# Whole-row loads of w_in, the first xT copies on GpSimd's queue, y copied by ScalarE alone, and another order of the first turn

## The chip, the cores and the metric

The kernel runs on one core of one Trainium2 chip. The metric is the device time of one execution in microseconds (us). Of the kernel before there are three timed executions, 340.52, 340.43 and 339.38 us, with a median of 340.43 us, and a fourth, profiled execution, from which every line of the profile comes.

## The reference, cut to what matters

A gated linear recurrence over 4 batches, 8 heads, 768 steps and 48 columns per head feeds a gated state-space block:

```python
for t in range(S):                                     # attention, per batch and head
    state = alpha[:, :, t, :, None] * state + k_t (outer) v_t
    y[:, :, t] = q_t @ state
x = y.transpose(0, 2, 1, 3).reshape(B, S, H * D)        # 4 x 768 x 384
proj = x @ w_in                                         # 384 x 1024
val, gate = proj[..., :512], proj[..., 512:]
h = exp(A_log) * h + val                                # running over the steps
out = (silu(gate) * hs) @ w_out                         # 512 x 384
```

`w_in` and `w_out` arrive as 64-bit floats (3.15 MB and 1.57 MB) and are turned into 32-bit ones on the chip.

## The kernel before, in words

The work is cut into N = 12 groups of 256 steps (three for each batch), each of two chunks of 128 steps. The function `fast` writes the order of every engine's instructions by hand; no scheduler moves them. An engine executes its own list strictly in order and waits, at each instruction, for what that one needs.

**The groups.** For a group m, q, k, v and alpha are loaded (groups 0 to 2 in "natural" layout by `load_natural`, L417, and turned by TensorE transposes `tn`, L563 and L574; later groups by `load_raw`, L396, and turned on VectorE, L597). VectorE runs two scans over alpha (`prod`, L606, and `inv`, L618) and scales q and k into Z (L580 or L629). TensorE makes the scores (L652) and the transposed keys (`tp`, L642), ScalarE and GpSimd mask them into A (L658 and L659; the other half is VectorE's L660), and TensorE makes y from A and v (L671), the state st (L692) and the part carried over from the chunk before (L682). `join(m)` (L697) copies the two halves of y out of PSUM into xT, one by ScalarE (L701) and one by VectorE (L702), and then moves six strips of 16 partitions within xT by six small DMAs (L705), three for each of the two engines named in its argument.

**The turns.** The loop at L821 runs over the groups' second part. Turn n multiplies xT of group n with w_in in four column blocks (`project(n, cc)`, L720: six matmuls for the values pv, six for the gates pg), runs the recurrence on VectorE (L727), applies Silu on ScalarE (`sg`, L732), multiplies the two on GpSimd (`f`, L733) and multiplies f with w_out (`output`, L741, sixteen matmuls). The last four of these wait for the fourth f. In the same turn the attention of group n+1 (scores to `join(n+1)`) and the scans of group n+2 are threaded between the four projections. Before the loop, group 0 and a part of group 1 are done.

**The weights.** `load_w` (L442) fetches w_in in three units by columns: unit 0 and unit 1 with 128 columns each for the values and the gates, unit 2 with 256 of each, every unit by eight DMAs (four of 48 rows times 3, four of 16 rows times 3), and w_out in two halves by one DMA of 128 partitions each (L456). The split into 48 and 16 rows is there because each head's 48 columns sit on the partitions 0 to 47 and 64 to 111, and what is left on 48 to 63 and 112 to 127. `convert(i)` (L506) makes 32-bit floats of one piece: one ScalarE instruction (`wr`, L518), two on VectorE (L519, L521) and one addition on GpSimd (L523), each over 768 elements a partition; `wr` has one buffer. There are six such pieces, four of w_in, one for each column block, and two of w_out. In turn 0 the six conversions stand at L814, L850, L867, L872, L893 and L895. `check_w` (L525) later reduces each loaded unit to a largest and a smallest value on VectorE, two reductions in each turn from turn 3 on.

**The queues.** SyncE (SP) issues nearly all loads in order. Each DMA's completion uses one of eight semaphores in rotation, shared by SP's and ScalarE's DMAs, and a DMA's issue waits for the one that used its semaphore before. So a load on SP can wait for a small xT copy that ScalarE issues later in the turn. In the profile, SPq and ACTq are SP and ScalarE issuing DMAs. `Lnnn` is a line of the kernel before.

Of the kernel before, what the change touches and what calls it, by code (L numbers as in the profile page):

```python
# [346 lines left out]
def fast(  # L347
# [87 lines left out]
    w_out = const.tile([C, NI, DM], FP32, name="w_out")  # L435

    W_UNITS = [(0, C), (C, C), (2 * C, 2 * C)]
    NW = 5
    wbits = [const.tile([C, NK, 2, w, 2], U32, name=f"wbits{i}") for i, (_, w) in enumerate(W_UNITS)]
    wbits += [const.tile([C, 2, 1, DM, 2], U32, name=f"wbits{i}") for i in range(3, NW)]  # L440

    def load_w(i, *engines):  # L442
        if i < 3:
            col, w = W_UNITS[i]
            src = moe_w_in.bitcast(U32)
            n = 0
            for rows in (((0, D, 0, D), (64, D, 4 * D, D)), ((D, R, 3 * D, R), (64 + D, R, 7 * D, R))):
                for vg in range(2):
                    for row, size, first, step in rows:
                        engines[n % len(engines)].dma_start(  # L450
                            out=wbits[i][ds(row, size), :, vg].rearrange("p kk n two -> p kk (n two)"),
                            in_=src[ds(first, NK * step), ds(2 * (vg * DI + col), 2 * w)]
                            .rearrange("(kk p) n -> p kk n", p=step)[0:size])
                        n += 1
        else:
            engines[0].dma_start(  # L456
                out=wbits[i].rearrange("p cc one n two -> p cc (one n two)"),
                in_=moe_w_out.bitcast(U32)[ds(2 * C * (i - 3), 2 * C)].rearrange("(cc p) n -> p cc n", p=C))
# [47 lines left out]
    def convert(i, part=0):  # L506

        if i < 3:
            bits = wbits[i][:, :, :, ds(part * C, C)]
            w = w_in[:, :, :, ds(W_UNITS[i][0] + part * C, C)]  # L510
        else:
            bits = wbits[i]
            w = w_out[:, ds(2 * (i - 3), 2), None, :]
# [4 lines left out]
        nc.scalar.activation(r, lo, AF.Copy, scale=2.0 ** -29)  # L518
        nc.vector.tensor_scalar(out=t, in0=hi, scalar1=3, scalar2=0x3FFFFFFF,  # L519
                                op0=ALU.logical_shift_left, op1=ALU.bitwise_and)  # L520
        nc.vector.scalar_tensor_tensor(out=t, in0=hi, scalar=0xC0000000, in1=t,  # L521
                                       op0=ALU.bitwise_and, op1=ALU.bitwise_or)
        return lambda: nc.gpsimd.tensor_tensor(out=w.bitcast(I32), in0=w.bitcast(I32), in1=r, op=ALU.add)  # L523

    def check_w(i):  # L525
        hi = wbits[i].rearrange("p a b n two -> p (a b n) two")[:, :, 1].bitcast(FP32)
        nc.vector.tensor_reduce(out=wmax[:, i:i + 1], in_=hi, axis=mybir.AxisListType.X, op=ALU.max,
                                apply_absolute_value=True)
        yield
        nc.vector.tensor_reduce(out=wmin[:, i:i + 1], in_=hi, axis=mybir.AxisListType.X, op=ALU.min,  # L530
                                apply_absolute_value=True)
        yield
# [164 lines left out]
    def join(m, engines):  # L697

        y = ys.pop(m)
        xT = xTs[m] = p2.tile([C, 4, GC], FP32, tag="xT", name="xT")  # L700
        nc.scalar.activation(xT[:, 1::2], y[1], AF.Copy)  # L701
        nc.vector.tensor_copy(out=xT[:, 0::2], in_=y[0])  # L702
        for s in range(2):
            for a in range(NK):
                engines[s].dma_start(out=xT[ds(64 * s + D, R), a], in_=xT[ds(64 * s + R * a, R), 3])  # L705
# [76 lines left out]
    load_w(2, SP)  # L782
    pair("a", 2, SP, SP)
    for i in range(3, NW):
        load_w(i, SP)
    pair("k", 2, SP, SP)
    pair("q", 2, SP, SP)

    warm = ps_mm.tile([C, 4, C], FP32, tag="mm", name="warm")
    for _ in range(5):  # L790
        nc.tensor.matmul(warm, ident, ident[:, None, :].to_broadcast([C, 4, C]), start=True, stop=True)
# [7 lines left out]
    for c in range(G):  # L799
        keys(0, c)  # L800
    for c in range(G):
        masks(0, c)
# [10 lines left out]
    join(0, (ACT, ACT))  # L813
    convert(0)()  # L814
    k_times, q_times = natural_qk(1, "k"), natural_qk(1, "q")
    for _ in steps:
        pass

    checks = itertools.chain.from_iterable(check_w(i) for i in range(NW))
    value = None  # L820
    for n in range(N):  # L821
# [24 lines left out]
        if n == 0:  # L846
            for c in range(G):
                k_times(c)
                q_times(c)
            convert(1)()  # L850
# [20 lines left out]
        if n == 0:  # L871
            convert(2, 1)()  # L872
# [3 lines left out]
        gated(n, 2, *pj)  # L876
        if not nat:
            go(2)
        if att:
# [6 lines left out]
            join(m, (ACT, ACT) if n < 2 else (SP, ACT))  # L886
        pj = project(n, 3)
        gated(n, 3, *pj)
        if nat:
            natural_alpha(n + 2)  # L890
            check_alpha(n + 2)
            go(2)
            convert(3)()  # L893
            go(1)
            convert(4)()  # L895
# [50 lines left out]
```

## Time and profile before

| what | value |
|---|---|
| median of three timed executions | 340.43 us (339.38 to 340.52) |
| profiled execution, its own time | 343.17 us |
| its span, first to last instruction | 341.4 us |
| mean granted TensorE clock | 0.935 of full |
| TensorE (PE) matmul busy | 297.5 us, 87% of the span |
| VectorE (DVE) busy | 232.3 us, 68% |
| GpSimd (POOL) busy | 105.5 us, 31% |
| ScalarE (ACT) busy | 91.7 us, 27% |
| DMA | 39.71 MB in 68269 packets, mean 116 GB/s |

All times in the profile's rows are us from the span's start. In a timeline row stand the start, the duration, the engine, the line, the operation, what it writes and reads with its shape, and how often; the bracket at the end gives how long the engine had been idle before and what ended that. In a row of the windows stand the stretch and its length, then the busy time of PE, PEld (TensorE's weight loads), DVE, ACT and POOL with the number of instructions, then the granted clock, the DMA share and GB/s. The profiled execution lies 2.74 us above the median of the timed ones, and 1.77 us of it lie outside the span.

### The profile page before, as it was taken

What the parts mean: (1) busy time and instruction counts of PE and PEld (TensorE: products, weight loads), DVE (VectorE), ACT (ScalarE), POOL (GpSimd) and SP (SyncE); (2) the same over time, 40 slices, a digit from 0 to 9 for tenths busy, and PEclk for the clock granted to TensorE, in tenths of its full rate; (3) what the DMA queues carried; (4) which work ended last, traced back from release to release, by engine and by line L of the source; (5) the groups of instructions that cost most, each with busy time, mean ns of one, the idle gap of its engine ahead of it and who ended that gap; (6) DMA issues with size and microseconds to landing.
All of it is one profiled execution on the core that took longest, in us unless ns stands there. A gap on an engine that the chain in (4) does not pass through costs nothing.

```text
span 341.4 us, 5950 instructions
## 1 busy us (share of the span) xinstructions
PE 297.5 (87%) x2341; PEld 234.5 (69%) x2341; DVE 232.3 (68%) x256; ACT 91.7 (27%) x188; POOL 105.5 (31%) x97
## 2 busy tenths in 40 slices
PE   3983869249997996899999999999999999999992
PEld 3572658116873883687886887878878788787771
DVE  3855671460896696389799899997998969643110
ACT  4161321311411421131411424214124152121111
POOL 6022272040251340072360611813516027041020
PEclk9997878757998999699999999999999999999997
DMA  9994996641406927980592956908739330100101
GB/s 134 181 170 91 187 265 137 167 69 48 113 0 145 239 55 140 225 141 12 154 205 65 239 76 163 202 15 216 144 99 222 60 94 3 38 22 13 47 4 54
DMA packets 68269, 39.71 MB, mean 116 GB/s; under 512 B 47364, under 2 KB 66952, under 8 KB 68232
## 3 DMA queue, kind: packets, MB, share of 16 engines
q1 hardware_dynamic: 65744, 38.30, 55.7%
q10 hardware_dynamic: 2488, 0.94, 1.3%
q8 instruction: 20, 0.33, 0.5%
q14 instruction: 17, 0.14, 0.1%
HBM read 33.33 MB, written 4.72 MB: 111 GB/s over the span
## 4 chain that ended last, share of the span: by engine, by line
PE 65%; DMA 10%; DVE 9%; SPq 6%; issue 4%; ACTq 2%; POOL 1%; ACT 1%; DVEq 0%; POOLq 0%
PE pv L720 17%; PE o L741 16%; PE pg L720 15%; PE sc L652 5%; DMA wbits<-in_moe_w_in_dram 5%; PE y L671 5%; PE y L682 2%; PE st L692 2%; SPq L420 2%; SPq L450 2%; ACTq L705 2%; PE tp L642 2%; DMA raw_k<-in_k_dram 2%; DVE prod L606 2%; DMA raw_q<-in_q_dram 1%
## 5 line engine op out<-in xcount | busy, mean ns | idle before, releaser
L733 POOL TENSOR_TENSOR f<-sg,hh 128x256 f32<-128x256 f32 x48 | 57.6, 1201 | 174.7 <-ACT sg L732 146.4
L720 PE MATMUL pv<-xT,w_in 128*128 128x256 f32 x288 | 77.7, 409 | 14.4 <-POOL w_in L523 10.1
L741 PE MATMUL o<-w_out,f 128*128 128x384 f32 x192 | 69.5, 516 | 13.9 <-POOL w_out L523 11.5
L720 PEld LDWEIGHTS pv<-xT,w_in 128*128 128x128 f32 x288 | 55.8, 201 | 28.5 <-POOL w_in L523 10.9
L720 PE MATMUL pg<-xT,w_in 128*128 128x256 f32 x288 | 73.3, 392 | 0.0
L741 PEld LDWEIGHTS o<-w_out,f 128*128 128x128 f32 x192 | 38.2, 201 | 40.0 <-POOL w_out L523 12.8
L720 PEld LDWEIGHTS pg<-xT,w_in 128*128 128x128 f32 x288 | 57.2, 199 | 8.6
L732 ACT ACTIVATE sg<-pg 128x256 f32<-128x256 f32 x48 | 18.4, 384 | 134.2 <-PE pg L720 84.2
L727 DVE TENSOR_TENSOR_SCAN hh<-a_dec,hh,pv 128x256 f32<-128x256 f32 x32 | 23.5, 735 | 42.5 <-PE pv L720 40.6
L659 POOL TENSOR_TENSOR A<-A,mask 128x512 f32<-128x512 f32 x24 | 32.0, 1354 | 30.2 <-ACT A L658 30.2
L606 DVE TENSOR_TENSOR_SCAN prod<-aT,first 128x1024 f32<-128x1024 f32 x12 | 32.8, 2734 | 0.1
L618 DVE TENSOR_TENSOR_SCAN inv<-aT,last 128x1025 f32<-128x1025 f32 x12 | 31.0, 2584 | 0.4
L652 PE MATMUL sc<-Z 48*128 48x128 f32 x384 | 25.1, 278 | 0.7 <-DVE Z L580 0.7
L671 PE MATMUL y<-A,v 128*64 128x128 f32 x384 | 23.9, 274 | 1.6 <-POOL A L659 1.6
L652 PEld LDWEIGHTS sc<-Z 48*128 48x128 f32 x384 | 22.7, 188 | 3.6 <-issue 2.2
L745 ACT ACTIVATE o_sb<-o 128x384 f32<-128x384 f32 x24 | 11.8, 491 | 48.6 <-PE o L741 48.6
L727 DVE TENSOR_TENSOR_SCAN hh<-a_dec,pv 128x256 f32<-128x256 f32 x16 | 10.9, 679 | 19.6 <-PE pv L720 19.4
L671 PEld LDWEIGHTS y<-A,v 128*64 128x64 f32 x384 | 20.7, 137 | 2.3 <-POOL A L659 2.1
L660 DVE TENSOR_TENSOR A<-sc,mask 128x512 f32<-128x512 f32 x24 | 16.4, 689 | 6.9 <-PE sc L652 6.6
L597 DVE STREAM_TRANSPOSE aT<-raw_a 128x1024 f32<-128x1024 f32 x9 | 18.3, 2038 | 0.0
L597 DVE STREAM_TRANSPOSE Z<-raw_q 128x1024 f32<-128x1024 f32 x9 | 18.3, 2036 | 0.0
L597 DVE STREAM_TRANSPOSE Z<-raw_k 128x1024 f32<-128x1024 f32 x9 | 18.2, 2018 | 0.0
(82 smaller groups left out, 249.8 us busy)
## 6 DMA issues: line engine op xcount, KB each, us to landing
raw_k<-in_k_dram SPq DMA_DIRECT2D x24, 192.0 KB, 5.0
raw_q<-in_q_dram SPq DMA_DIRECT2D x24, 192.0 KB, 5.2
v<-in_v_dram SPq DMA_DIRECT2D x24, 192.0 KB, 4.4
out_dram<-o_sb SPq DMA_DIRECT2D x24, 192.0 KB, 1.9
raw_a<-in_alpha_dram SPq DMA_DIRECT2D x23, 192.0 KB, 4.0
raw_a<-in_alpha_dram SPq DMA_DIRECT2D x18, 176.0 KB, 4.0
raw_k<-in_k_dram SPq DMA_DIRECT2D x18, 176.0 KB, 5.1
raw_q<-in_q_dram SPq DMA_DIRECT2D x18, 176.0 KB, 4.0
```

What stands on the lines that cost most here:

```text
L597: nc.vector.transpose(out=to.rearrange("p h (c j) -> p h j c", j=NT), in_=raw_bufs[m % NR][name].rearrange("p h (j d) -> p h j d", d=D)[:, ...
L606: nc.vector.tensor_tensor_scan(out=prod, data0=aT[:, 0:4 * GC], data1=first.rearrange("p h n -> p (h n)"), initial=0.0, op0=ALU.mult, op1= ...
L618: nc.vector.tensor_tensor_scan(out=inv[:, ::-1], data0=aT[:, ::-1], data1=last.rearrange("p h n -> p (h n)")[:, 0:4 * GC + 1][:, ::-1], in ...
L652: nc.tensor.matmul(sc[i][:, p, :], Z[rows, p, 1, cols], Z[rows, p, 0, cols], start=True, stop=True)
L659: nc.gpsimd.tensor_mul(A[:, 1], A[:, 1], mb)
L660: nc.vector.tensor_mul(A[:, 0], sc[0], mb)
L671: nc.tensor.matmul(ys[m][i][ds(64 * s, 64), e, ds(c * C, C)], v_sb[:, c, 2 * p + i, :], A[:, i, p, :], start=(c == 0 and e == 0), stop=Fal ...
L720: nc.tensor.matmul(pj, w_in[:, kk, vg, ds(cc * C, C)], xT[:, kk, :], start=(kk == 0), stop=(kk == NK - 1))
L727: nc.vector.tensor_tensor_scan(out=hh, data0=a_dec[:, cc:cc + 1].to_broadcast([C, GC]), data1=pv, initial=prev_h[cc][:, GC - 1:GC] if g el ...
L732: nc.scalar.activation(sg, pg, AF.Silu)
L733: nc.gpsimd.tensor_mul(fs[n][:, cc, :], sg, hh)
L741: nc.tensor.matmul(os[c], fs[n][:, cc, ds(c * C, C)], w_out[:, cc, :], start=(cc == 0), stop=(cc == NI - 1))
```

## The change

Five things are changed, all in `fast`:

- `load_w_in` fetches w_in once, in four DMAs of whole rows (48 or 16 partitions, 3 rows of 8 KB each), where there were 24. They stand where unit 0's eight DMAs stood on SP. w_out follows behind k and q of group 1, v of group 1 behind that, and then a, k and q of group 2.
- `join(0)` and `join(1)` issue their six small DMAs on GpSimd's queue and no longer on ScalarE's; `join(2)` uses SP and ScalarE, as the later groups do in both kernels.
- Both copies of y in `join` are ScalarE's, in every group.
- `convert` works on one column block of w_in or one half of w_out at a time (i = 0 to 5) and `wr` has two buffers. The conversions are put in other places of turn 0: the fourth block behind project(0, 1), both halves of w_out behind project(0, 2), where they had stood behind project(0, 3) and the scans of group 2. The scaling of k and q of group 1 (L580) goes ahead of project(0, 0); it stood behind it. Group 0's masks go ahead of its keys. A second set of five matmuls on a constant (`warm`) is put behind group 0's y.
- `check_w` goes by rows of w_in (three units of 1024 elements a partition) and halves of w_out (two of 768); before, it was units of 768, 768, 1536, 768 and 768.

The diff, cut to its core:

```diff
-    W_UNITS = [(0, C), (C, C), (2 * C, 2 * C)]
...
+    bits_in = const.tile([C, NK, 2 * DI, 2], U32, name="bits_in")
+    bits_out = const.tile([C, NI, DM, 2], U32, name="bits_out")
+    def load_w_in(engine):
+        for row, size, first, step in ((0, D, 0, D), (64, D, 4 * D, D), (D, R, 3 * D, R), (64 + D, R, 7 * D, R)):
+            engine.dma_start(out=bits_in[ds(row, size)].rearrange("p kk n two -> p kk (n two)"),
+                             in_=moe_w_in.bitcast(U32)[ds(first, NK * step)]
+                             .rearrange("(kk p) n -> p kk n", p=step)[0:size])
...
-        r = p1.tile([C, x, y, z], I32, tag="wr", name="wr")
+        r = p2.tile([C, x, y, z], I32, tag="wr", name="wr")
...
         nc.scalar.activation(xT[:, 1::2], y[1], AF.Copy)
-        nc.vector.tensor_copy(out=xT[:, 0::2], in_=y[0])
+        nc.scalar.activation(xT[:, 0::2], y[0], AF.Copy)
...
-    load_w(0, SP)
+    load_w_in(SP)
     pair("k", 1, SP, SP)
     pair("q", 1, SP, SP)
-    load_w(1, SP)
+    for i in range(2):
+        load_w_out(i, SP)
     load_v(1, SP)
...
-    join(0, (ACT, ACT))
+    join(0, (nc.gpsimd, nc.gpsimd))
     convert(0)()
+    warm()
     k_times, q_times = natural_qk(1, "k"), natural_qk(1, "q")
     for _ in steps:
         pass
+    for c in range(G):
+        k_times(c)
+        q_times(c)
...
         if n == 0:
-            convert(2, 1)()
+            convert(3)()
...
         pj = project(n, 2)
         gated(n, 2, *pj)
+        if n == 0:
+            convert(4)()
+            convert(5)()
...
-            join(m, (ACT, ACT) if n < 2 else (SP, ACT))
+            join(m, (nc.gpsimd, nc.gpsimd) if n == 0 else (SP, ACT))
...
-            convert(3)()
-            go(1)
-            convert(4)()
```

SP's loads behind v of group 0, before (`wbits_88` to `wbits_90` are the three units of w_in, `wbits_91` and `wbits_92` the halves of w_out; `raw_k_83`, `raw_q_82` and `v_85` belong to group 1, `raw_a_78` here to group 2):

```order
L429 DMA v_84<-in_v_dram 128x8x48 x2
L450 DMA wbits_88<-in_moe_w_in_dram 48x3x256 x4
L450 DMA wbits_88<-in_moe_w_in_dram 16x3x256 x4
L420 DMA raw_k_83<-in_k_dram 128x8x48 x2
L420 DMA raw_q_82<-in_q_dram 128x8x48 x2
L450 DMA wbits_89<-in_moe_w_in_dram 48x3x256 x4
L450 DMA wbits_89<-in_moe_w_in_dram 16x3x256 x4
L429 DMA v_85<-in_v_dram 128x8x48 x2
L450 DMA wbits_90<-in_moe_w_in_dram 48x3x512 x4
L450 DMA wbits_90<-in_moe_w_in_dram 16x3x512 x4
L420 DMA raw_a_78<-in_alpha_dram 128x8x48 x2
L456 DMA wbits_91<-in_moe_w_out_dram 128x2x768
```

and the same place now, on SP:

```order
L429 DMA v_84<-in_v_dram 128x8x48 x2
L443 DMA bits_in<-in_moe_w_in_dram 48x3x2048 x2
L443 DMA bits_in<-in_moe_w_in_dram 16x3x2048 x2
L420 DMA raw_k_83<-in_k_dram 128x8x48 x2
L420 DMA raw_q_82<-in_q_dram 128x8x48 x2
L448 DMA bits_out<-in_moe_w_out_dram 128x2x768 x2
L429 DMA v_85<-in_v_dram 128x8x48 x2
L420 DMA raw_a_78<-in_alpha_dram 128x8x48 x2
```

All of w_in now stands ahead of k and q of group 1, and w_out ahead of everything of group 2.

ScalarE in turn 0, before, from the conversion of the third column block on (`y_509` is group 1's y; `sg` are the Silus of turn 0):

```order
L518 ACTIVATE wr<-wbits_90 128x768
L732 ACTIVATE sg<-pg 128x256
L518 ACTIVATE wr<-wbits_90 128x768
L732 ACTIVATE sg<-pg 128x256
L695 ACTIVATE S_sb<-st 128x192 x2
L701 ACTIVATE xT<-y_509 128x2x256
L705 DMA xT<-xT 16x256 x6
L732 ACTIVATE sg<-pg 128x256
L564 ACTIVATE aT<-tn 128x4x128 x2
L591 ACTIVATE junk,above<-raw_a_78,minus 128x768
L518 ACTIVATE wr<-wbits_91 128x768
L518 ACTIVATE wr<-wbits_92 128x768
```

and the same place now:

```order
L510 ACTIVATE wr<-bits_in 128x768
L725 ACTIVATE sg<-pg 128x256
L510 ACTIVATE wr<-bits_in 128x768
L725 ACTIVATE sg<-pg 128x256
L510 ACTIVATE wr<-bits_out 128x768 x2
L688 ACTIVATE S_sb<-st 128x192 x2
L694 ACTIVATE xT<-y_502 128x2x256
L695 ACTIVATE xT<-y_501 128x2x256
L725 ACTIVATE sg<-pg 128x256
L557 ACTIVATE aT<-tn 128x4x128 x2
```

The two conversions of w_out have moved ahead of group 1's y, its six DMAs have left ScalarE, and a second copy has come.

GpSimd over the same stretch, before, from group 0's masks on:

```order
L659 TENSOR_TENSOR A<-A,mask 128x512 x2
L523 TENSOR_TENSOR w_in<-w_in,wr 128x6x128
L733 TENSOR_TENSOR f<-sg,hh 128x256
L523 TENSOR_TENSOR w_in<-w_in,wr 128x6x128
L659 TENSOR_TENSOR A<-A,mask 128x512 x2
L523 TENSOR_TENSOR w_in<-w_in,wr 128x6x128
L733 TENSOR_TENSOR f<-sg,hh 128x256
L523 TENSOR_TENSOR w_in<-w_in,wr 128x6x128
L733 TENSOR_TENSOR f<-sg,hh 128x256 x2
L523 TENSOR_TENSOR w_out<-w_out,wr 128x768 x2
```

and now:

```order
L652 TENSOR_TENSOR A<-A,mask 128x512 x2
L698 DMA xT<-xT 16x256 x6
L515 TENSOR_TENSOR w_in<-w_in,wr 128x6x128
L726 TENSOR_TENSOR f<-sg,hh 128x256
L515 TENSOR_TENSOR w_in<-w_in,wr 128x6x128
L652 TENSOR_TENSOR A<-A,mask 128x512 x2
L515 TENSOR_TENSOR w_in<-w_in,wr 128x6x128
L726 TENSOR_TENSOR f<-sg,hh 128x256
L515 TENSOR_TENSOR w_in<-w_in,wr 128x6x128
L726 TENSOR_TENSOR f<-sg,hh 128x256
L515 TENSOR_TENSOR w_out<-w_out,wr 128x768 x2
L698 DMA xT<-xT 16x256 x6
```

GpSimd now issues twelve DMAs. The second six stand ahead of turn 0's fourth f, the additions for w_out as well.

More of the change, by code (lines that the diff above doesn't have):

```diff
@@ L435, in fast, with load_w_out @@
     w_out = const.tile([C, NI, DM], FP32, name="w_out")
-    W_UNITS = [(0, C), (C, C), (2 * C, 2 * C)]
[L438 to L458, printed above, removed]
+    NW = NK + 2
+    bits_in = const.tile([C, NK, 2 * DI, 2], U32, name="bits_in")
[5 more added lines that the diff above has]
+                             .rearrange("(kk p) n -> p kk n", p=step)[0:size])
+    def load_w_out(i, engine):
+        engine.dma_start(out=bits_out[:, ds(2 * i, 2)].rearrange("p cc n two -> p cc (n two)"),
+                         in_=moe_w_out.bitcast(U32)[ds(2 * C * i, 2 * C)].rearrange("(cc p) n -> p cc n", p=C))
     one = const.tile([C, 1], FP32, name="one")
@@ L525, in check_w @@
     def check_w(i):
[L526 to L532, printed above, removed]
+        if i < NK:
+            hi = bits_in[:, i, :, 1].bitcast(FP32)
+        else:
+            hi = bits_out[:, ds(2 * (i - NK), 2)].rearrange("p cc n two -> p (cc n) two")[:, :, 1].bitcast(FP32)
+        for t, op in ((wmax, ALU.max), (wmin, ALU.min)):
+            nc.vector.tensor_reduce(out=t[:, i:i + 1], in_=hi, axis=mybir.AxisListType.X, op=op,
+                                    apply_absolute_value=True)
+            yield
     def check_end():
@@ L781, in fast, with warm @@
     k_times, q_times = natural_qk(0, "k"), natural_qk(0, "q")
[L782 to L791, printed above, removed]
+    for name in "akq":
+        pair(name, 2, SP, SP)
+    def warm():
+        t = ps_mm.tile([C, 4, C], FP32, tag="mm", name="warm")
+        for _ in range(5):
+            nc.tensor.matmul(t, ident, ident[:, None, :].to_broadcast([C, 4, C]), start=True, stop=True)
+    warm()
     for _ in products(0):
@@ L799, in fast @@
     for c in range(G):
+        masks(0, c)
+    for c in range(G):
         keys(0, c)
-    for c in range(G):
-        masks(0, c)
     natural_alpha(1)
```

18 lines of the change are left out of this document (8 added, 10 removed).

## The prediction

> **What bounds the kernel now.** I read the windows of the span first, cut at the first projection of each turn. The columns are the stretch, its length, then the busy time of PE, PEld, DVE, ACT and POOL, the granted clock, the DMA share and GB/s. Here are turns 0, 1, 2, 3, 5, 6 and 9:
>
> ```profile
> 33.11:84.66 51.55, 35.57 (x224) 26.16 (x225) 23.70 (x27) 12.27 (x22) 14.67 (x11) 0.73 0.71 145
> 84.66:110.47 25.81, 22.88 (x182) 17.57 (x181) 21.47 (x22) 5.88 (x12) 7.76 (x6) 0.97 0.37 87
> 110.47:138.15 27.68, 23.37 (x186) 18.51 (x184) 18.94 (x18) 7.45 (x16) 6.92 (x6) 0.93 0.70 147
> 138.15:163.35 25.20, 25.20 (x200) 20.23 (x201) 19.52 (x20) 6.42 (x14) 8.96 (x6) 0.90 0.59 118
> 185.07:207.25 22.18, 22.18 (x186) 17.95 (x185) 19.97 (x20) 6.97 (x16) 6.91 (x6) 1.00 0.71 143
> 207.25:230.94 23.69, 23.22 (x203) 18.74 (x202) 22.71 (x22) 7.30 (x17) 8.89 (x6) 1.00 0.60 135
> 274.83:297.44 22.61, 22.61 (x201) 18.39 (x201) 18.33 (x18) 6.96 (x16) 9.00 (x6) 1.00 0.17 40
> ```
>
> From turn 4 on TensorE has no idle time worth the name (22.18 busy of 22.18, 22.61 of 22.61): nothing but fewer matmuls would shorten those turns. All that the change can win lies ahead of them. Turn 0 takes 51.55 us with 16 us of idle PE and a clock of 0.73. Groups repeat by threes, since a batch has three, so turn 2 compares with turn 5 (27.68 against 22.18), and turns 3 and 6 with turn 9 (25.20 and 23.69 against 22.61).
>
> The timeline of turn 0 tells what PE waits for at its end:
>
> ```profile
> 70.61 2.93 PE L741 MATMUL o<-w_out,f 128*128 128x384 f32 x4 [8.85 <-POOL w_out L523]
> 74.30 1.80 POOL L523 TENSOR_TENSOR w_out<-w_out,wr 128x768 int32<-128x768 int32 x1 [3.74 <-DVE w_out L521]
> 76.15 6.93 PE L741 MATMUL o<-w_out,f 128*128 128x384 f32 x12 [2.61 <-POOL w_out L523]
> ```
>
> Two waits of 8.85 and 2.61 us are for w_out's conversion, which stands behind group 1's join and group 2's scans. After the first the matmuls are slow as well.
>
> **The change, part by part. Loads.** Rates, from finer windows: loads of the natural layout alone, w_in alone (unit 2, in DMAs of 48 and 16 partitions), and w_out alone (128 partitions):
>
> ```profile
> 8.00:10.00 2.00, 2.00 (x12) 2.00 (x11) 0.89 (x3) 1.85 (x4) 0.00 (x0) 1.00 1.54 163
> 36.00:38.00 2.00, 2.00 (x8) 1.58 (x7) 1.92 (x4) 0.00 (x0) 0.00 (x0) 0.64 1.08 199
> 46.00:48.00 2.00, 0.00 (x0) 0.00 (x0) 2.00 (x3) 0.02 (x1) 1.30 (x1) 0.92 1.03 399
> v<-in_v_dram SPq DMA_DIRECT2D x24, 192.0 KB, 4.4
> ```
>
> Whole rows make the runs 8 KB, but keep the split into 48 and 16 partitions, so I keep 199 GB/s. The ends are 163 (the lowest full-share row) and 399. [...]
>
> Ten natural loads of 192 KB (1.97 MB) at 163 from 2.0 us end at 14.1. Then 3.15 MB at 199 take 15.8 us, to 29.9, and k and q of group 1 (0.79 MB at 163) 4.8, to 34.7. With their landing and the last transposes, about 1.5 us by estimate, the first projection can start at 36.2, where it now starts at 33.11: whole rows, ahead of k and q, cost 3.1 us. The 20 issues saved on SP bring nothing, since the DMA engines are the limit. The w_out data come by about 39 (1.57 MB at 399), v of group 1 by 42, a, k and q of group 2 by 49, all ahead of their use below.
>
> **The first join.** Its rows now, and those of the first block's work behind it:
>
> ```profile
> 25.66 0.66 DVE L702 COPY xT<-y 128x512 f32<-128x512 f32 x1
> 26.39 3.79 ACTq L705 DMA_DIRECT2D xT<-xT  x6
> 30.29 0.89 ACT L518 ACTIVATE wr<-wbits 128x768 int32<-128x768 uint32 x1 [4.49 <-DMA xT<-xT]
> 31.26 1.80 POOL L523 TENSOR_TENSOR w_in<-w_in,wr 128x768 int32<-128x768 int32 x1 [8.00 <-ACT wr L518]
> 33.11 2.93 PE L720 MATMUL pv<-xT,w_in 128*128 128x256 f32 x6 [5.65 <-POOL w_in L523]
> 38.13 0.38 ACT L732 ACTIVATE sg<-pg 128x256 f32<-128x256 f32 x1 [6.95 <-PE pg L720]
> 39.18 2.06 PE L652 MATMUL sc<-Z 48*128 48x128 f32 x32
> 42.64 2.51 POOL L659 TENSOR_TENSOR A<-A,mask 128x512 f32<-128x512 f32 x2
> ```
>
> Six issues take ScalarE 3.79 us, 0.63 each. On GpSimd no row shows one. The nearest is this same transfer, so I take 0.63. The lower end is nothing at all, the upper end a DMA that waits for a whole VectorE instruction, 3.77 us (below, third rival). At 0.63 the first six end by 30.2, ahead of 36.2, and cost nothing; the cover is the wait for q of group 1. [...]
>
> **Turn 0.** Its other prices, from the timeline and, for a warm pair pv and pg and for the output, from the chain of waits:
>
> ```profile
> 53.97 0.90 PE L692 MATMUL st<-v,ktm 128*64 128x48 f32 x16
> 54.54 0.73 POOL L733 TENSOR_TENSOR f<-sg,hh 128x256 f32<-128x256 f32 x1 [2.27 <-ACT sg L732]
> 58.04 1.56 PE L720 MATMUL pv<-xT,w_in 128*128 128x256 f32 x6
> 83.79 1.04 PE L574 MATMUL tn<-ident,raw_q 128*128 128x128 f32 x8
> ```
>
> ```profile
> 117.11 1.49 PE pv L720 x6
> 118.60 1.29 PE pg L720 x6
> ...
> 128.67 5.17 PE o L741 x16
> ```
>
> From the start at 36.2: first projection (cold) with keys and scores, 8.1 (33.11 to 41.24), to 44.3. Second projection 2.8, to 47.1. The third waits for its block: Silu at 36.2 + 5.0 = 41.2, then 0.4, `wr` 0.9, the second addition 1.8, the masks 2.5 and the third addition 1.8, to 48.6. Projection 2.8, to 51.4; state and y 4.1, to 55.5; fourth projection 2.8, to 58.3; alpha's transposes 1.0, to 59.3; output 5.2, to 64.5; transposes of k and q of group 2, 2.1, to 66.6. So turn 1 starts at 66.6, where it now starts at 84.66: 18.1 us less.
>
> What covers the rest: the additions for w_out follow the third f on GpSimd (51.8 + 0.7 + 3.6 = 56.1), ahead of the output at 59.3. ScalarE's two copies of y end by 56.7, and the second six DMAs at 60.5. The fourth f then ends at 61.2, ahead of the last four output matmuls at 63.2. Up to 0.9 us per DMA costs nothing there; each 0.1 more costs 0.6.
>
> **Turns 1 to 3.** These rows show how ScalarE's join of group 2 ends turn 1, and how the shared join of group 3 ends turn 2:
>
> ```profile
> 99.36 0.60 ACT L701 ACTIVATE xT<-y 128x512 f32<-128x512 f32 x1 [3.17 <-PE y L682]
> 102.90 3.72 ACTq L705 DMA_DIRECT2D xT<-xT  x6
> 108.41 2.26 PE L741 MATMUL o<-w_out,f 128*128 128x384 f32 x4 [2.48 <-POOL f L733]
> ...
> 128.46 1.80 ACTq L705 DMA_DIRECT2D xT<-xT  x3
> 130.24 2.02 SPq L405 DMA_DIRECT2D raw_q<-in_q_dram  x4
> 133.52 2.95 SPq L705 DMA_DIRECT2D xT<-xT  x3
> 138.15 2.90 PE L720 MATMUL pv<-xT,w_in 128*128 128x256 f32 x6 [4.31 <-issue]
> ```
>
> In turn 2 SP's load of q waits until ScalarE's first xT DMA has landed (128.46 to 130.24), and SP's own xT DMAs stand behind it: 9.7 us from ScalarE's first issue to the next projection, of which PE idles 4.31. Now group 2's join is the shared one, and the order of the semaphores puts the same wait into turn 1. ScalarE copies both halves back to back (99.36 + 1.2 = 100.6, which is 15.9 into the turn), its Silu no longer stands behind six issues, and the 2.48 us of the output go. But 15.9 + 9.7 = 25.6: turn 1 takes 25.6 against 25.81, a gain of 0.2. The stall has only another cause. In turn 2 the semaphores fall as in the steady turns, so its stall goes; it starts with a slow clock, though, as this row after an idle of only 2.48 us shows:
>
> ```profile
> 110.00:112.00 2.00, 2.00 (x6) 1.41 (x5) 0.00 (x0) 0.49 (x1) 0.00 (x0) 0.50 0.90 218
> ```
>
> The price of such a start is turn 3 against turn 9, 2.6 us. Turn 2 becomes 22.18 + 2.6 = 24.8, a gain of 2.9, and turn 3, which starts warm, gains 2.6.
>
> **Steady turns.** VectorE loses a copy of 0.66 us a turn and ScalarE gains one of 0.60; ScalarE is busy 7 of 22 us, and PE waits for neither. Turn 6 is 1.1 longer than turn 9, and this reduction is why:
>
> ```profile
> 206.85 1.75 DVE L527 TENSOR_REDUCE wmax<-wbits 128x1 f32<-128x1536 f32 x1
> ```
>
> Two of them delay turn 6's recurrence. With 1024 elements (two thirds, 1.17 by estimate) and the copy gone the delay goes: 1.1 less. The second set of warming matmuls falls into the wait for k and q and costs nothing.
>
> **Sum.** 18.1 + 0.2 + 2.9 + 2.6 + 1.1 = 24.9 us. The profiled execution of 343.17 becomes 318.3, its span of 341.4 becomes 316.5. It lay 2.7 above the median of the timed runs; taken off the median of 340.43, I predict 315.5 us.
>
> **The rivals.** *w_in at full rate.* If 8 KB runs go at 399 GB/s, w_in takes 7.9 us and q lands at 26.8. Then GpSimd sets the start (26.39 + 3.8 + 1.8 = 32.0): 4.2 less, 311.3 us. Against it stands 199 at 2 KB, with only the run's length different now. Chance 0.12.
>
> *w_in slower.* Four long loads may fill the DMA engines unevenly, where 24 short ones alternate between the two halves of the partitions. At 163 GB/s they take 19.3 us: 3.5 more, 319.0 us. Nothing in the trace shows long 48-row loads. Chance 0.18. [...]
>
> *GpSimd's DMAs held up by VectorE: slower than before.* GpSimd and VectorE disturb each other: the first f of turn 0 above takes 0.73, the mean of the page's row is 1.20. If each DMA had to wait for a whole VectorE instruction like this scan,
>
> ```profile
> 68.94 3.77 DVE L618 TENSOR_TENSOR_SCAN inv<-aT,last 128x1025 f32<-128x1025 f32 x1
> L733 POOL TENSOR_TENSOR f<-sg,hh 128x256 f32<-128x256 f32 x48 | 57.6, 1201 | 174.7 <-ACT sg L732 146.4
> ```
>
> the first six would take 22.6 us and start turn 0 at 50.8 (14.6 late). The second six, from 56.7 + 14.6, end at 93.9; product, last matmuls and transposes (4.1) give 98.0 for turn 1, 13.3 later than now. With the other gains of 6.8 that is 346.9 us. It decides from 3.2 us per DMA (52.8 + 12 x 3.2 = 91.2, against 84.66 + 6.8). Against it: the mean product loses half a microsecond to its neighbours, not three. Chance 0.04. [...]
>
> **Chances and range.** The forecast as worked out, within about 3 us, has 0.60. The three rivals have 0.34. The remaining 0.06 is GpSimd's DMAs at one to three us, between forecast and before. A measurement of this kernel can tell about 0.5%, 1.7 us, from no change. Only the third rival and a part of the last case reach that side: faster 0.94, same 0.02, slower 0.04. The range reaches down to the first rival with turn 2's cold start (2.6) and the 1.5 us for landings spared, 307, and up to the second rival with GpSimd's DMAs at 1.5 us each as well ((1.5 - 0.9) x 6 = 3.6, 322.6), about 322.
>
> **What would show it.** Right: the first projection near 36 us and behind the transposes of q; turn 1 starting near 67; no wait of PE for w_out; GpSimd's six DMAs within 4 us; turn 1 still near 25.6 with a wait for xT at its end; turn 6 like turn 9. Wrong: w_in landing near 22 or past 33 us, gaps between GpSimd's DMAs as long as VectorE's instructions, or turn 0 longer than 33 us for a wait that is not in the sum.

## The result, and the profile after

| | before | after |
|---|---|---|
| median of four timed executions | 339.94 us (339.38 to 340.52) | 328.69 us (327.42 to 330.93) |
| profiled execution | 343.17 us | 330.93 us |
| its span | 341.4 us | 329.2 us |
| its mean granted clock | 0.935 | 0.957 |

The ratio is 0.9676, with a 95% interval from 0.9618 to 0.9734: faster, but by 11 us and not by the 25 forecast. The median lies 13.2 us above the predicted 315.5 and 6.7 above the upper end of the range. The profiled executions tell the same: 330.93 against 318.3 forecast, 12.6 us too much.

The windows of the kernel after, cut at the first projection of each turn (same columns as in the prediction), show everything ahead of turn 0, then turns 0, 1, 2 and 6:

```profile
0.00:45.83 45.83, 26.21 (x190) 18.85 (x190) 19.68 (x29) 11.76 (x21) 12.57 (x28) 0.84 1.14 150
45.83:78.16 32.33, 29.04 (x226) 22.88 (x225) 24.87 (x27) 12.41 (x23) 20.28 (x17) 0.91 0.91 165
78.16:103.93 25.77, 22.11 (x183) 17.21 (x181) 20.85 (x21) 6.85 (x14) 8.15 (x6) 0.98 0.57 121
103.93:129.12 25.19, 25.19 (x184) 20.16 (x185) 18.25 (x17) 6.91 (x15) 6.91 (x6) 0.88 0.53 120
195.63:218.24 22.61, 22.61 (x202) 18.39 (x201) 20.34 (x21) 7.45 (x17) 9.00 (x6) 1.00 0.67 141
```

Turn 0 took 51.55 us before and now takes 32.33, turns 1, 2 and 6 come out as forecast within 0.4, and the steady turns are full. But the first projection, which stood at 33.11 and was forecast at 36.2, starts at 45.83. Those 9.6 us are most of the miss. (Some 1.5 us of it is spread: in g2 and h2 below, whose instructions are the same up to there, it starts at 45.13 and 44.28.) The timeline ahead of that start names the cause:

```profile
10.66 2.75 SPq L443 DMA_DIRECT2D bits_in<-in_moe_w_in_dram  x4
13.45 13.09 SPq L420 DMA_DIRECT2D raw_k<-in_k_dram  x2
26.59 14.36 SPq L420 DMA_DIRECT2D raw_q<-in_q_dram  x2
...
40.37 0.91 ACT L510 ACTIVATE wr<-bits_in 128x768 int32<-128x768 uint32 x1 [15.67 <-DMA bits_in<-in_moe_w_in_dram]
41.16 1.12 PE L567 MATMUL tn<-ident,raw_k 128*128 128x128 f32 x4 [13.15 <-DMA raw_k<-in_k_dram]
45.83 2.77 PE L713 MATMUL pv<-xT,w_in 128*128 128x256 f32 x6
```

w_in is issued within 2.75 us from 10.66 on, but ScalarE's first conversion waits for it until 40.37, and the issues of k and q stand on SP for 13.09 and 14.36 us. Behind w_in follow the transposes of k and q, and behind them the projection, as forecast; only the time is another. Three windows while w_in is moved give its rate in the last column:

```profile
16.00:24.00 8.00, 7.84 (x128) 7.05 (x129) 4.51 (x7) 5.22 (x11) 2.50 (x2) 1.00 1.01 134
24.00:34.00 10.00, 4.01 (x10) 1.50 (x8) 0.00 (x0) 0.69 (x2) 3.07 (x6) 0.87 1.02 131
34.00:38.00 4.00, 0.00 (x0) 0.00 (x0) 0.00 (x0) 0.00 (x0) 0.00 (x0) 0.50 0.97 110
```

It is 131 to 134 GB/s, and 110 at the end, where I took 199 and bounded it below by 163. In whole-row form w_in is slower than the lowest row on which the prediction drew.

### The profile page after: what moved, and what is told of

It reads as the page before. It is cut to its first block, busy times and chain, and to the rows that moved or that the text cites. A ratio compares the mean times of both kernels' runs of the same rounds, so it can differ in the third digit from the quotient of the medians.

```text
span 329.2 us, 5980 instructions
## 1 busy us (share of the span) xinstructions
PE 296.0 (90%) x2351; PEld 234.3 (71%) x2351; DVE 228.0 (69%) x244; ACT 97.2 (30%) x200; POOL 114.4 (35%) x109
## 4 chain that ended last, share of the span: by engine, by line
PE 73%; SPq 8%; DMA 7%; DVE 5%; POOL 4%; issue 1%; ACT 0%; POOLq 0%; DVEq 0%
PE pv L713 19%; PE o L734 18%; PE pg L713 17%; SPq L420 6%; PE sc L645 6%; DMA raw_q<-in_q_dram 5%; PE y L664 5%; PE y L675 3%; PE st L685 2%; PE tp L635 2%; POOL A L652 1%; POOL f L726 1%; DVE w_out L513 1%; PE tn L567 1%; DMA raw_a<-in_alpha_dram 1%; SPq L443 1%
## 5 line engine op out<-in xcount | busy, mean ns | idle before, releaser
L726 POOL TENSOR_TENSOR f<-sg,hh 128x256 f32<-128x256 f32 x48 | 60.1, 1252 | 155.0 <-ACT sg L725 133.4
L713 PE MATMUL pv<-xT,w_in 128*128 128x256 f32 x288 | 76.5, 404 | 6.3 <-DMA xT<-xT 3.2
L713 PE MATMUL pg<-xT,w_in 128*128 128x256 f32 x288 | 71.7, 386 | 0.0
L713 PEld LDWEIGHTS pv<-xT,w_in 128*128 128x128 f32 x288 | 55.0, 198 | 19.5 <-issue 5.8
L734 PE MATMUL o<-w_out,f 128*128 128x384 f32 x192 | 64.3, 487 | 0.2 <-POOL f L726 0.2
L713 PEld LDWEIGHTS pg<-xT,w_in 128*128 128x128 f32 x288 | 56.2, 195 | 8.1
L734 PEld LDWEIGHTS o<-w_out,f 128*128 128x128 f32 x192 | 36.2, 190 | 23.3 <-POOL f L726 0.8
L590 DVE STREAM_TRANSPOSE aT<-raw_a 128x1024 f32<-128x1024 f32 x9 | 18.3, 2036 | 0.0
L590 DVE STREAM_TRANSPOSE Z<-raw_q 128x1024 f32<-128x1024 f32 x9 | 18.3, 2033 | 0.0
```

The lines of the kernel that those rows point to most:

```text
L590: nc.vector.transpose(out=to.rearrange("p h (c j) -> p h j c", j=NT), in_=raw_bufs[m % NR][name].rearrange("p h (j d) -> p h j d", d=D)[:, ...
L713: nc.tensor.matmul(pj, w_in[:, kk, vg, ds(cc * C, C)], xT[:, kk, :], start=(kk == 0), stop=(kk == NK - 1))
L726: nc.gpsimd.tensor_mul(fs[n][:, cc, :], sg, hh)
L734: nc.tensor.matmul(os[c], fs[n][:, cc, ds(c * C, C)], w_out[:, cc, :], start=(cc == 0), stop=(cc == NI - 1))
```

## The experiments

**How w_in is best loaded (four runs, one time each, the kernel before at 339.14 us beside them).** Two theories. *Halves*: a DMA of 48 rows writes only one half of the partitions, and long ones run one after another, so what counts is whether the two halves come in alternation. *Run length*: 8 KB runs are slow by themselves. The first two runs cut w_in into the same 16 DMAs with 2 KB runs and differ in order alone.

e1_pieces_alternate, column quarters outside, row groups inside:

```diff
-        for row, size, first, step in ((0, D, 0, D), (64, D, 4 * D, D), ...):
-            engine.dma_start(out=bits_in[ds(row, size)]...
+        for col in range(4):
+            for row, size, first, step in ((0, D, 0, D), (64, D, 4 * D, D), ...):
+                engine.dma_start(out=bits_in[ds(row, size), :, ds(256 * col, 256)]...
```

> w_in at the same place in SP's queue, in 16 DMAs of 2 KB runs, going in turn over the four row groups (0 to 47, 64 to 111, 48 to 63, 112 to 127) for each quarter of the columns. The theory of the halves says that a DMA of 48 partitions writes to one half of the partitions only, and that the two halves work side by side only where short DMAs alternate between them: w_in takes about 16 us (199 GB/s as before the change) where the change took 26.7 (13.6 to 40.3), the first projection starts near 36 where it started at 45.8, and the time falls by about 9.6 us to 319. The theory of the run length says that runs of 8 KB are slower than runs of 2 KB: the same numbers here. If w_in still takes about 26 us, both are wrong.

Measured: 321.33 us. The window while w_in moves, and the first projection:

```profile
16.00:24.00 8.00, 7.80 (x128) 7.03 (x128) 4.62 (x7) 5.12 (x11) 2.50 (x2) 1.00 1.08 193
...
37.80 1.67 PE L714 MATMUL pv<-xT,w_in 128*128 128x256 f32 x6
```

e2_pieces_by_rows, the same two loops exchanged (`for row, ...` outside, `for col` inside):

> The same 16 DMAs of 2 KB runs, in another order: all four quarters of the partitions 0 to 47 first, then of 64 to 111, then of 48 to 63 and of 112 to 127. Halves: as slow as the change, about 26 us for w_in, first projection near 45.8, 328.7 us. Run length: as fast as with alternating pieces, 16 us, first projection near 36, about 319 us.

Measured: 328.47 us.

```profile
16.00:24.00 8.00, 7.82 (x128) 7.03 (x128) 4.54 (x7) 5.20 (x11) 2.51 (x2) 1.00 1.07 164
...
42.16 1.46 PE L714 MATMUL pv<-xT,w_in 128*128 128x256 f32 x6
```

e3_rows_alternate keeps the 8 KB runs, but cuts each DMA into its three rows a partition and lets the row groups alternate:

```diff
+        for kk in range(NK):
+            for row, size, first, step in ((0, D, 0, D), (64, D, 4 * D, D), ...):
+                engine.dma_start(out=bits_in[ds(row, size), kk]...
```

> Whole rows of 8 KB as in the change, but one row for each partition and DMA: 12 DMAs that go in turn over the four row groups. Halves: near 16 us for w_in, 20 at most since the pieces are longer than in the alternating quarters (393 KB against 295), first projection at 36 to 40, 319 to 323 us. Run length: 26 us, first projection near 45.8, 328.7 us.

Measured: 320.95 us. The third row is the third projection, for later:

```profile
16.00:24.00 8.00, 7.79 (x128) 7.02 (x128) 4.67 (x7) 5.07 (x11) 2.51 (x2) 1.00 1.01 182
...
38.44 2.18 PE L713 MATMUL pv<-xT,w_in 128*128 128x256 f32 x6
50.92 1.56 PE L713 MATMUL pv<-xT,w_in 128*128 128x256 f32 x6 [2.68 <-POOL w_in L515]
```

e4_all_partitions loads w_in by one DMA of 128 partitions:

```diff
+        engine.dma_start(out=bits_in.rearrange("p kk n two -> p kk (n two)"),
+                         in_=moe_w_in.bitcast(U32).rearrange("(kk p) n -> p kk n", p=C))
```

> One DMA of whole rows to all 128 partitions (3 rows of 8 KB each), which puts w_in's rows in another order than x's columns, so the product with w_in is not the reference's. Halves: all of the partitions at once as in w_out's DMAs, 399 GB/s, 8 us for w_in, q of group 1 lands near 27, first projection at 31 to 33, 314 to 316 us. Run length: 26 us or more, first projection near 45.8.

Measured: 314.07 us.

```profile
16.00:22.00 6.00, 5.83 (x90) 5.51 (x92) 2.85 (x7) 4.34 (x9) 2.51 (x2) 1.00 1.01 396
...
32.70 2.23 PE L711 MATMUL pv<-xT,w_in 128*128 128x256 f32 x6 [2.94 <-DMA xT<-xT]
```

What follows: with 2 KB runs, alternation gives 193 GB/s and no alternation 164; with 8 KB runs, 182 and 134. From 13.6 or 13.7 us, where the loads ahead have landed, to the landing of its last DMA, w_in takes 18.3 us in e1, 23.5 in e2, 18.9 in e3 and 26.7 after the change. So the order is most of the cause, and long runs by themselves are not: e3 with 8 KB is nearly as fast as e1 with 2 KB. But the cutting counts as well where nothing alternates: e2 saves some 3 us of w_in against the changed kernel and starts its first projection at 42.16 in place of 45.83. Its one time of 328.47 shows no gain over the changed kernel's median, though it is 2.5 below that kernel's profiled execution. So both theories missed a part. e1 itself came 2.3 us above its forecast, with 18.3 us for w_in where 16 were expected. One DMA over all partitions gets 396. In every run that alternates, the next DMA goes to the other half and also to other partitions, so that it is the halves that count is argued and not shown. What lies behind the difference isn't in a profile either; both stay open. The split into 48 and 16 rows cannot be given up for e4's form, since the columns of x lie on the partitions by heads.

**The change without whole rows, and whole rows alone.** g1_old_units puts the old column units, at their old places between the other loads, into the changed kernel (the third unit and w_out go back to their places among group 2's loads as well):

```diff
-    load_w_in(SP)
+    load_w_in(SP, 0, C)
     pair("k", 1, SP, SP)
     pair("q", 1, SP, SP)
-    for i in range(2):
-        load_w_out(i, SP)
+    load_w_in(SP, C, C)
     load_v(1, SP)
...
```

> The changed kernel in all but one thing: w_in comes in the old column units again (eight short DMAs a unit that alternate between the two halves of the partitions, in the old places between the other loads), into the new tile. Theory (only w_in's long loads were mis-sized, and a later first projection is paid one for one): k and q of group 1 land by about 24 us as before the change, the first projection starts at 32 to 33.5 in place of 45.83, turn 0 takes 32 to 35 (the third block waits for the last unit, which lands near 44), turn 1 starts at 65 to 67 in place of 78.05, and the whole takes 315.5 to 318.5 us. Rival (the early start is given back: the units and w_out land too late for a turn 0 of 32 us, so PE waits for the conversion of w_in or w_out): turn 0 takes over 40 us and the whole 324 to 329.

Measured: 326.27 us (325.46 to 329.12) beside 339.06 for the kernel before, ratio 0.9631 (0.9555 to 0.9707). Neither theory fits: the first projection did not start early.

```profile
41.55 0.91 ACT L513 ACTIVATE wr<-bits_in 128x768 int32<-128x768 uint32 x1 [16.69 <-DMA bits_in<-in_moe_w_in_dram]
45.10 2.93 PE L716 MATMUL pv<-xT,w_in 128*128 128x256 f32 x6 [15.19 <-POOL w_in L518]
```

The first conversion waits for a DMA of w_in until 41.55, when the last DMA of the last unit has just landed (41.53); those of the first unit were in by 19.2. My edit had loaded the units into slices of the one tile `bits_in`, and the conversion waited for all of it. So this run says nothing of the rate. h1_unit_tiles is the same with a tile for each unit (`bits_in[i]`, as the kernel before had, and with it that kernel's reductions by units):

> The run g1 again, with a tile for each unit of w_in, so that the conversion of the first block waits for the first unit alone (in g1 the one tile made it wait for the last unit, at 41.5 us). Theory (a later first projection is paid one for one, and w_in's long loads are its only cause): first projection at 33 to 34.5, set by the landing of GpSimd's xT DMAs (33.65 in g1), turn 0 of 32 to 35 us since the third block waits for the last unit, turn 1 at 66 to 69 in place of 78.05, the whole 317 to 320.5 us. Rival (given back: w_in's last unit and w_out then hold up turn 0): turn 0 over 40 us, the whole 324 to 329.

Measured: 318.54 us (316.22 to 320.88) beside 339.88, ratio 0.9384 (0.9337 to 0.9431).

```profile
24.66 0.92 ACT L514 ACTIVATE wr<-bits_in 128x768 int32<-128x768 uint32 x1
31.14 0.67 PE L717 MATMUL pv<-xT,w_in 128*128 128x256 f32 x2 [1.31 <-DMA xT<-xT]
31.14:63.78 32.64, 28.03 (x225) 21.90 (x225) 21.26 (x23) 12.43 (x23) 19.16 (x17) 0.95 1.06 213
```

The conversion runs at 24.66, the first projection starts at 31.14 (even before the 33 expected), turn 0 takes 32.64, hardly longer than with whole rows, and turn 1 starts at 63.78. In the profiled executions nothing is given back: the first projection stands 14.7 us earlier than after the change, turn 1 starts 14.4 earlier. In the medians the gain is 10.2 us (328.69 - 318.54); the profiled execution of h1 was the fastest of its six, that of the changed kernel the slowest of its four. The 10.2 us are the price of four long DMAs ahead of k and q, not of their order alone, since in h1 the first block also waits for its own unit only, and k and q go ahead of the rest of w_in. e1 and e3, which change nothing but the cutting and the order, save 7.4 and 7.7 us by their one time each.

g4_rows_in_old is the other side, the kernel before with the whole-row load (and, since w_in is one tile then, the reductions by rows) as its only change:

```diff
-    wbits = [const.tile([C, NK, 2, w, 2], U32, name=f"wbits{i}") for i, (_, w) in enumerate(W_UNITS)]
+    bits_in = const.tile([C, NK, 2 * DI, 2], U32, name="bits_in")
+    whole = bits_in.rearrange("p kk (vg n) two -> p kk vg n two", vg=2)
+    wbits = [whole[:, :, :, ds(col, w)] for col, w in W_UNITS]
...
+            if i:
+                return
+            for row, size, first, step in ((0, D, 0, D), (64, D, 4 * D, D), ...):
+                engines[0].dma_start(out=bits_in[ds(row, size)]...
```

> The kernel before with one part of the change alone: w_in in four DMAs of whole rows, at the place of its first unit. All else, the conversions and the orders and the queues too, as before the change. Theory (the four long loads run one after another on one half of the partitions each, at about 131 GB/s, and hold up k and q of group 1): w_in in by about 40 us, first projection at 45 to 47 in place of 33.11; turn 0, which waited for later units of w_in and for w_out, gets 3 to 10 us shorter than its 51.55; the whole takes 343 to 350 us, slower than before by 1 to 3 per cent. The xT DMAs of the first join, here from ScalarE, land after 11 to 14 us by theory A and after 2 by theory B of the run before. Rival (whole rows are only slow beside GpSimd's DMAs, or pay back in turn 0 all that they cost): w_in in by 33, or the whole within 1.5 us of 340 or below.

Measured: 353.16 us (351.27 to 354.01), ratio 1.0422 (1.0332 to 1.0511): slower, and 3 us above the upper end expected.

```profile
45.66 2.67 PE L721 MATMUL pv<-xT,w_in 128*128 128x256 f32 x6
81.03 2.93 PE L742 MATMUL o<-w_out,f 128*128 128x384 f32 x4 [8.58 <-POOL w_out L520]
45.66:95.20 49.54, 33.66 (x225) 24.43 (x225) 24.15 (x28) 12.42 (x22) 16.32 (x11) 0.77 0.58 117
```

The first projection starts 12.6 later than before the change, and turn 0 gets only 2.0 shorter (49.54 against 51.55), where 3 to 10 were expected, since its wait of 8.58 us for w_out's conversion is there as before. This part of the change costs, and the other parts bring all of the gain.

**The queues of the joins.** g3_joins_scalar puts groups 0 and 1 back on ScalarE:

```diff
-    join(0, (nc.gpsimd, nc.gpsimd))
+    join(0, (ACT, ACT))
...
-            join(m, (nc.gpsimd, nc.gpsimd) if n == 0 else (SP, ACT))
+            join(m, (ACT, ACT) if n == 0 else (SP, ACT))
```

> The changed kernel with the joins of groups 0 and 1 back on ScalarE's queue. On the time: theory (as forecast, GpSimd's queue spares turn 0 the six issues of the second join that hold up the last Silu; the first join is hidden either way): 1.5 to 4 us longer than 328.7, so 330 to 333, with a wait of PE for f near 2.5 us at turn 0's output. Rival (hidden in both): within 1 us. On the landing of the first six xT DMAs, 13.3 to 13.9 us on GpSimd's queue while w_in's 8 KB packets are in flight: theory A (each transfer waits its turn behind long packets in the DMA engines, whichever queue it comes from): 11 to 14 us from ScalarE as well. Theory B (GpSimd's queue itself is slow then): about 2 us from ScalarE, as before the change.

Measured: 330.78 us (328.58 to 332.29), ratio 0.975 (0.9663 to 0.9838). It is 2.1 above the changed kernel in the medians, but the intervals of the two ratios overlap, so the whole alone does not decide. The timeline does:

```profile
67.87 3.96 ACTq L698 DMA_DIRECT2D xT<-xT  x6
71.88 0.38 ACT L725 ACTIVATE sg<-pg 128x256 f32<-128x256 f32 x1 [4.04 <-issue]
72.41 7.09 PE L734 MATMUL o<-w_out,f 128*128 128x384 f32 x16 [2.06 <-ACT sg L725]
```

The Silu stands behind six issues, the output behind the Silu by 2.06 us, and its sixteen matmuls take 7.09, where the changed kernel's take 5.60 (4.04 and 1.56). That is what GpSimd's queue takes away: turn 0 takes 36.72 us here (44.36 to 81.08) against 32.33. The whole differs by less, since in this execution the first projection stands 1.5 us earlier (44.36 against 45.83) and turn 2 is 1.2 shorter (23.95 against 25.19). The first six xT DMAs landed 10.2 us after their issue: below theory A's 11 to 14, and far from theory B's 2.

g2_third_join_gpsimd gives GpSimd the join of group 2 as well (`if n <= 1` in the line above):

> The changed kernel with one more join, that of group 2, wholly on GpSimd's queue in place of ScalarE's and SP's. Theory (turn 1's stall of 3.22 us is SP's load of q that waits for ScalarE's xT DMA, with SP's own xT DMAs behind it; the slow start of turn 2 follows from the idle): turn 1 takes 22.3 to 23.3 in place of 25.9, turn 2 22.2 to 23.0 in place of 25.3, and the whole is 4 to 6 us shorter than the changed kernel's 328.7, so 322.5 to 325. Rival (the stall goes with the first join that is shared, whichever it is): turn 1 gets shorter, but the wait for xT now ends turn 2 and the cold start falls on turn 3, so the whole stays within 1.5 us of 328.7.

Measured: 328.41 us (327.43 to 329.07), ratio 0.9693 (0.9615 to 0.9771), no change: the rival was right. Turn 1 shrinks to 22.4, but the stall now ends turn 2:

```profile
115.32 1.86 ACTq L698 DMA_DIRECT2D xT<-xT  x3
117.17 2.03 SPq L405 DMA_DIRECT2D raw_q<-in_q_dram  x4
120.62 2.66 SPq L698 DMA_DIRECT2D xT<-xT  x3
125.33 2.16 PE L713 MATMUL pv<-xT,w_in 128*128 128x256 f32 x6 [3.27 <-DMA xT<-xT]
```

h2_joins_gpsimd therefore gives GpSimd all joins (`join(m, (nc.gpsimd, nc.gpsimd))`):

> The changed kernel with every join's xT DMAs on GpSimd's queue, none shared by ScalarE and SP. After the run g2 the theory is: the stall falls on whichever join is the first to be shared, by SP's load of q that waits for ScalarE's xT DMA; with no shared join there is none. Turn 1 22.4 as in g2, and turn 2 22 to 22.6 as well, the whole 6 to 7 us shorter than the changed kernel's 328.7: 321.5 to 323. Rival 1 (the stall comes from how the loads and the joins fall in time, not from sharing): a wait for xT of about 3 us remains in one of turns 1 to 3, the whole within 1.5 us of 328.7. Rival 2 (GpSimd's six issues of 3 us in each turn hold up its products): the steady turns get longer by 0.3 us or more each, and of the gain less than 4 us is left.

Measured: 323.49 us (321.75 to 324.69), ratio 0.9515 (0.9468 to 0.9562). Turns 1 and 2:

```profile
76.25:98.65 22.40, 21.95 (x183) 17.37 (x182) 20.75 (x21) 6.31 (x13) 10.38 (x12) 1.00 0.64 132
98.65:120.82 22.17, 22.17 (x185) 17.95 (x184) 18.37 (x18) 7.44 (x17) 9.87 (x12) 1.00 0.69 143
```

Both are at their steady length and the granted clock stays at 1.00. The medians differ by 5.2 us, somewhat less than the 6 to 7 expected; the two turns account for 6.4 (25.77 + 25.19 - 22.40 - 22.17). Turn 2 of the changed kernel was at the long end, though: in e1, e2, e3, g1, g3, h1 and h4, with a stall ahead of it too, it took 23.7 to 25.0 us. The later turns do not suffer from GpSimd's issues: turns 3 to 9 take 21.72 to 22.61 us here and 21.72 to 22.62 in the changed kernel.

h3_units_and_joins is h1 and h2 together:

> The two edits h1 and h2 together. Theory (they act at different places, before turn 0 and at the end of turn 1, so they add up): about 10 + 6.5 us less than the changed kernel, 311 to 314 us. Rival (TensorE's granted clock falls or loads come late when the first turns are packed more closely): at least 4 us of the sum is missing, 316 us or more.

Measured: 313.34 us (310.99 to 314.34) beside 339.88, ratio 0.9193 (0.9143 to 0.9243). The two add up, and this kernel beats both.

**The copies of y.** h4_y_vector puts y[0] back on VectorE (`nc.vector.tensor_copy(out=xT[:, 0::2], in_=y[0])`):

> The changed kernel with the copy of y[0] back on VectorE, in every turn. Theory (as forecast: the copy costs nothing in the steady turns on either engine, save the delay of turn 6's recurrence that the shorter reductions took away too): within 1 us of 328.7. Rival (the freed 0.66 us a turn on VectorE is what made the steady turns even): turns 4 to 10 longer by 0.2 us or more each, 330.5 to 333.

Measured: 331.6 us (329.5 to 331.9), ratio 0.9733 (0.9686 to 0.978), with an interval that overlaps the changed kernel's. The theory's 1 us is exceeded by the medians. It is the rival's time, but not by its mechanism: turns 4 to 10 are as long as after the change (turn 6 stays at 22.61). What is longer is the end of turn 1, 28.10 us, where the changed kernel and the seven other runs with its join of group 2 and its copies (e1 to e4, g1, g3, h1) have 24.5 to 26.0.

```profile
94.00 0.66 DVE L695 COPY xT<-y 128x512 f32<-128x512 f32 x1
94.74 1.86 ACTq L698 DMA_DIRECT2D xT<-xT  x3
104.61 2.90 PE L713 MATMUL pv<-xT,w_in 128*128 128x256 f32 x6 [5.11 <-DMA xT<-xT]
```

VectorE comes to this copy at 94.00, behind a transposition of 2.01 us from 92.14 on; the shared join's chain starts from it, and PE waits 5.11 us where it waits 3.22 after the change.

## Why the prediction was wrong in size and right in most steps

**The loads: wrong, 9.6 of the 12.6 us.** The step that failed reads "Whole rows make the runs 8 KB, but keep the split into 48 and 16 partitions, so I keep 199 GB/s." The 199 came from unit 2, whose short DMAs alternate between the halves. The partitions of each DMA were kept, but not the alternation, and that is what most of the rate hangs on (193 GB/s in e1 against 164 in e2, 182 in e3 against 134 in the changed kernel). So w_in was in at 40.3 where the sum had 29.9, 10.4 us late; what stands behind it took 5.6 us to the first projection where the sum had 6.3. I had this as the second rival, at 0.18, but took as its bound the lowest row in sight, 163 GB/s, which belongs to another layout; it gave 319.0, and the truth was slower than any row there. The four long loads, issued within 2.75 us, landed at 24.18, 34.17, 37.93 and 40.26; from 13.6, where the loads ahead of them have ended, w_in took some 26.7 us, where that rival had 19.3. In e1 and e3, where short ones alternate, 182 to 193 GB/s were reached. Why a long DMA of 48 rows moves no more than this, no run shows.

**Turn 0: right but for 1.9 us.** 30.4 was forecast, 32.33 measured. The third projection waits as forecast, but runs slowly after the wait:

```profile
58.72 2.93 PE L713 MATMUL pv<-xT,w_in 128*128 128x256 f32 x6 [2.69 <-POOL w_in L515]
58.72:61.44 2.72, 2.72 (x6) 2.19 (x7) 1.73 (x2) 0.00 (x0) 1.76 (x2) 0.50 1.05 230
61.44 1.80 PE L713 MATMUL pg<-xT,w_in 128*128 128x256 f32 x6
```

The granted clock is 0.50 in this stretch, and the pair takes 4.5 us (58.72 to 63.2) where the sum had 2.8. In e3 the same wait of 2.68 us is followed by a projection of 1.56, and there turn 0 takes 30.6 (38.44 to 69.00), the forecast's 30.4. I had priced a cold start in turn 2 and forgotten it here.

**The first join and GpSimd's issues: right.** Forecast at 0.63 us each, within 4 us for six. Measured, issues and then (from the DMA view) the median from issue to landing:

```profile
25.00 3.07 POOL L698 DMA_DIRECT2D xT<-xT  x6 [4.42 <-ACT xT L695]
...
69.28 2.93 POOL L698 DMA_DIRECT2D xT<-xT  x6
...
xT<-xT POOLq DMA_DIRECT2D x6, 16.0 KB, 13.8
...
xT<-xT POOLq DMA_DIRECT2D x6, 16.0 KB, 1.7
```

That is 0.5 us each, no gaps. But VectorE is idle during the first six and for most of the second six, so these rows alone do not put the third rival out. h2 does: this join stands beside VectorE at work all through (a transposition, a scan and a product), takes as long, and the next projection, which starts at 98.65, 3.4 us after the last issue, has no wait for it:

```profile
92.33 2.94 POOL L698 DMA_DIRECT2D xT<-xT  x6 [2.51 <-ACT xT L695]
```

That the first six took 13.8 us to land was not foreseen; it stays hidden behind k and q, but without w_in's delay it would not: in h1 and e4 the first projection waits for just these (1.31 and 2.94 us).

**Turn 0's cover: right, with less to spare.** No wait of PE for w_out remains, and the fourth f costs the output only 0.17 us. The sum had 2.0 us to spare there; the fourth f itself took 2.73 us, beside a scan on VectorE, where the sum had 0.7:

```profile
72.23 2.73 POOL L726 TENSOR_TENSOR f<-sg,hh 128x256 f32<-128x256 f32 x1
75.02 1.56 PE L734 MATMUL o<-w_out,f 128*128 128x384 f32 x4 [0.17 <-POOL f L726]
```

**Turns 1 to 3: right.** 25.6, 24.8 and 22.6 were forecast; 25.77, 25.19 and 22.62 (129.12 to 151.74) came. The stall is where and what the forecast said:

```profile
93.97 1.86 ACTq L698 DMA_DIRECT2D xT<-xT  x3
95.83 2.00 SPq L405 DMA_DIRECT2D raw_q<-in_q_dram  x4
99.28 3.06 SPq L698 DMA_DIRECT2D xT<-xT  x3
103.93 2.90 PE L713 MATMUL pv<-xT,w_in 128*128 128x256 f32 x6 [3.22 <-DMA xT<-xT]
```

Runs g2 and h2 add what the forecast left open: it falls on the first shared join in each of the kernels before, after and g2 (4.31, 3.22 and 3.27 us of idle PE), and costs 5.0 to 6.4 us with the slow start behind it (turns 1 and 2 of g3 and of the changed kernel against h2's). Why the later shared joins do not stall, no run shows.

**Turn 6: right, but worth 0.7 and not 1.1 us.** 22.61, as turn 9. The prediction's row for turn 6 of the kernel before ends at 230.94, and turn 7 starts at 230.55; cut there, the turn was 23.30 long:

```profile
207.25:230.55 23.30, 22.83 (x202) 18.37 (x201) 22.32 (x22) 7.07 (x16) 8.89 (x6) 1.00 0.61 137
```

The forecast asked for shorter reductions and the moved copy together, and each is enough alone: with short reductions and y[0]'s copy on VectorE (h4, g4) turn 6 takes 22.61, with the old reductions of 1.75 us and both copies on ScalarE (h1) 22.63. With this the 12.6 us add up within 0.1: 9.6 ahead of turn 0, 1.9 in it, 0.2 and 0.4 in turns 1 and 2, and the 0.4 that turn 6 did not have to give. The copies on ScalarE, which I gave no separate price, are worth about 2 us at turn 1's end (28.10 in h4 against 25.77).

## What to carry to other kernels

In these runs the DMA rate belonged to the pattern in which the transfers follow one another more than to a single transfer's run length: the loads here that cover part of the partitions were fastest when issued short and in alternation between the two groups of partitions (193 against 164 GB/s with 2 KB runs, 182 against 134 with 8 KB), and fewer, longer DMAs were no gain where that order was lost (in g4 the first projection came 12.6 us later). Whatever was queued behind such a load (here k and q, whose issues stood on SP for 13.09 and 14.36 us, and with them the first projection) was late by it. Where a stall came from two engines whose DMAs share their semaphores, moving one join away only handed it to the next (3.27 us in g2 after 3.22 in the changed kernel); taking the sharing away altogether ended it (h2, no wait ahead of turns 2 and 3).

## What the runs showed of the hardware that was not expected

The small DMAs of the first join landed late while w_in was in flight, from GpSimd's queue and from ScalarE's: the first six of 16 KB took 13.8 us to land after the change (9.9 in e2, 8.3 in e3, 7.4 in e1), the second six, behind w_in, 1.7 us. From ScalarE's queue, in g3 and g4, it was 10.2 and 10.1 us, so most of it isn't GpSimd's doing; what makes up the other 3.6 us stays open. The 1.9 us of the kernel before is no measure for this, since hardly anything else was in flight there (8 GB/s from 26 to 28 us).

```profile
xT<-xT ACTq DMA_DIRECT2D x6, 16.0 KB, 10.2
```

The DMA share in the windows was 1.01 to 1.08 at 134, 164, 193 and 396 GB/s alike, so the share did not tell these rates apart. And the same idle of 2.7 us of TensorE was followed once by a clock of 0.50 (the changed kernel, turn 0) and once by one of 1.00 (e3, 50.92 to 53.50); why, the runs do not tell.
